# Local attention in a fused attention and expert kernel: the score products of two heads alternate, and a small add moves from VectorE to GpSimd

## The chip, the cores and the metric

The kernel runs on one core of a Trainium2 chip. The metric is device microseconds per execution; the time of a kernel is the median of several runs. In the profile PE is TensorE (PEld its weight loads), DVE VectorE, ACT ScalarE, POOL GpSimd and SP SyncE, whose queue issues the loads and copies.

## The reference, cut to what matters

Four batches of eight heads have 512 local and 32 global tokens, with 64 numbers per head. A local token attends to the 32 global tokens and to the local ones at most 32 places away; a global token attends to all. Two feed-forward stages follow.

```python
s_ll = scale * np.matmul(q_l, k_l.transpose(0, 1, 3, 2))
s_ll = np.where(np.abs(pos[:, None] - pos[None, :]) <= 32, s_ll, -1e9)
s_l = np.concatenate([scale * np.matmul(q_l, k_g.transpose(0, 1, 3, 2)), s_ll], axis=-1)
# sm(s): e = exp(s - max(s)); e / (sum(e) + 1e-9)
out_l = np.matmul(sm(s_l), np.concatenate([v_g, v_l], axis=2))
x = out.transpose(0, 2, 1, 3).reshape(2176, 512)
x = np.square(np.maximum(x @ w_in, 0)) @ w_out                 # first feed-forward
P = sinkhorn(softmax-like gate of x, 8 rounds)                  # 8 experts
out = sum over e of P[:, e] * (np.maximum(x @ w1[e], 0) @ w2[e])
```

Inputs and output are 32-bit floats; some of the attention's inputs are scaled up, so that the scores are large.

## The kernel before, in words

Every product is made of three: each operand is split into a rounded part (`hi`) and what is left (`lo`), and `split_terms` gives hi x hi, hi x lo and lo x hi, which TensorE adds up in PSUM.

The attention comes first, up to about 215 us. It goes over 16 items: a batch and a pair of heads. The two heads of a pair lie side by side on the partitions, head 0 on 0 to 63 and head 1 on 64 to 127 (`halves`). Each item has two local steps of two tiles of 128 queries each (`qp`), and every second item a global step for the queries of the global tokens of two pairs. So five steps make a period: local, local, local, local, global.

The order of the work is written out by hand: each engine does its instructions in the order in which the loop at L659 issues them. In turn `k` of that loop several steps are at different points. First comes `loc_normalise` of step k-2 (L491), then `loc_least` of step k-1 (masking, and the smallest negated score of each row, L469), then on ScalarE and VectorE the evacuations from PSUM that the turn before left behind (`evacuate_all`, L361; `hi` by ScalarE at L363 or L365, `lo` by VectorE at L368 or L370), `loc_exp` of k-1 (L483), `loc_values` of k-4 (L519), `loc_scores` of k (L458) and `loc_transpose` of k-2 (L506). In some turns there follow the transposes of the next item's keys and queries, `prep_v` (L426: GpSimd splits the values at L80 and L81, and copies go out on the queue of SP) and, every second item, `glob_queries` (L535: four copies on GpSimd, L121). Last, `step_side` works on the weights of the first feed-forward stage, a few operations of ScalarE, VectorE and GpSimd at a time (`double_words`, L98 to L108; `split_words`, L113 to L117).

What the change touches: `loc_scores` takes two PSUM tiles "s", one per head, from a pool of two. For each head it makes three products for each of the two tiles of queries, 12 in all, each with 64 rows, 128 queries and 224 keys (L466). `loc_exp` leaves four sums of exponentials in `st[:, 4:8]`. `loc_normalise` adds the constant 1e-9 to them (L493) and takes the reciprocal (L494), both on VectorE; GpSimd then scales the four blocks of exponentials in place (L497), which TensorE transposes later in the same turn.

There are 32 local steps, so L493 and L494 run 32 times and L466 384 times.

Of the kernel before, what the change touches and what calls it, by code (L numbers as in the profile page):

```python
# [9 lines left out]
F32 = mybir.dt.float32  # L10
# [3 lines left out]
ALU = mybir.AluOpType  # L14
# [4 lines left out]
EPS = 1e-9  # L19
# [3 lines left out]
def split_terms(hi_s, lo_s, hi_m, lo_m):  # L23


    return ((hi_s, hi_m), (hi_s, lo_m), (lo_s, hi_m))
# [3 lines left out]
def kernel(  # L30
# [15 lines left out]
    nc = tc.nc  # L46
# [4 lines left out]
    E, _, F2 = w1.shape  # L51
    P = 128
# [5 lines left out]
    SEG = P + 3 * WINDOW  # L58
# [199 lines left out]
    with ExitStack() as actx:  # L258
# [3 lines left out]
        pss = actx.enter_context(tc.tile_pool(name="pss", bufs=2, space=PSUM))  # L262
# [190 lines left out]
        halves = (slice(0, D), slice(D, 2 * D))  # L453
        s_t, e_t, pt_t, st_t, inv_t = {}, {}, {}, {}, {}
# [2 lines left out]

        def loc_scores(i, n, qp):  # L458
            q, kt = QT[n], KT[n % 3]
            s_t[i] = []  # L460
            for r in halves:
                s = pss.tile([P, 2, SEG], F32, tag="s", name="s")
                for t in range(2):
                    qt = 2 * qp + t
                    for x, (a, c) in enumerate(split_terms(q[r, 0, qt], q[r, 1, qt], kt[r, 0, qt], kt[r, 1, qt])):
                        nc.tensor.matmul(s[:, t, :], lhsT=a, rhs=c, start=(x == 0), stop=(x == 2))  # L466
                s_t[i].append(s)

        def loc_least(i, n, qp):  # L469
            e = ap3.tile([P, 2, 2, SEG], F32, tag="e", name="e")  # L470
# [19 lines left out]

        def loc_normalise(i):  # L491
            e, st = e_t[i], st_t.pop(i)
            nc.vector.tensor_scalar_add(st[:, 4:8], st[:, 4:8], EPS)  # L493
            nc.vector.reciprocal(st[:, 4:8], st[:, 4:8])  # L494
            for c in range(4):
                v = e[:, c // 2, c % 2, :]
                nc.gpsimd.tensor_scalar(out=v, in0=v, scalar1=st[:, 4 + c : 5 + c], scalar2=1.0, op0=ALU.mult, op1=ALU.mult)  # L497
# [161 lines left out]
        for k in range(len(steps) + 6):  # L659
            if k < len(steps):  # L660
                kind, n, qp = steps[k]
                first, second = kind == "l" and qp == 0, kind == "l" and qp == 1
                closing = steps[k + 1][:1] + steps[k + 1][2:] == ("l", 0) if k + 1 < len(steps) else False
            else:
                first = second = closing = False
            at(k - 2, loc_normalise, glob_normalise)
            if 0 <= k - 1 < len(steps):
                kd, m, mq = steps[k - 1]
# [9 lines left out]
            at(k - 1, loc_exp, glob_exp)  # L678
            at(k - 4, loc_values, glob_values, 1)
            at(k, loc_scores, glob_scores, 1)  # L680
            if len(steps) <= k < len(steps) + 4:
                step_early(2)
# [31 lines left out]
            if first and n == 15:  # L714
                add_part(share, 1, 0, "kg")
                t = share.tile([P, 3, 512], F32R, tag="kt1", name="w20")
# [5 lines left out]
            if k == len(steps):  # L722
                add_part(share, 3, 0, "vb1")
                t = share.tile([P, 3, 512], F32R, tag="kt2", name="w31")
# [350 lines left out]
    for u in range(U1):  # L1075
        if u and u < U1 - 1:
            prepare((u + 1) * UF)
        if u == U1 - 1:
            t = cv.tile([P, 6, 512], F32, tag="cv", name="t").rearrange("p a b -> p (a b)")[:, 0 : 8 * P]
            t = t.rearrange("p (i k f) -> p i k f", i=4, k=2)  # L1080
# [47 lines left out]
    for tb, (j0, nj) in enumerate(TBS):  # L1128
        n = nj * P // 2
        for u in range(NS):  # L1130
            s = tb * NS + u
# [57 lines left out]
```

## Time and profile before

| | us |
|---|---|
| median of 3 runs | 2042.18 (2038.86 to 2042.25) |
| the profiled execution's own time | 2037.85 |
| its span, first to last instruction | 2035.9 |

| engine | busy us | share of the span | instructions |
|---|---|---|---|
| PE | 1997.6 | 98% | 10820 |
| DVE | 1210.8 | 59% | 2398 |
| ACT | 807.9 | 40% | 1856 |
| POOL | 922.6 | 45% | 1071 |

The share is an average over stages: in the first tenth of the span the page gives VectorE nine tenths and more, afterwards about half. TensorE's clock was granted in full for nearly all of the span (0.992 on average). Matmuls are pipelined, and their ends are modelled, so a busy TensorE is not one at its peak.

### The profile page before, as it was taken

How to read it: one execution, taken by the hardware profiler on the slowest of the kernel's cores; microseconds unless marked ns; L12 is line 12 of the kernel's file. 1: busy time of each engine (PE TensorE's matmuls, PEld its weight loads, DVE VectorE, ACT ScalarE, POOL GpSimd, SP SyncE). 2: the span in 40 equal slices, each digit the busy share in tenths (PEclk: the TensorE clock that was granted, in tenths of full speed). 3: DMA queues.
4: the chain of work that ended last, by engine and by line, in shares of the span. 5: the costliest groups of instructions: out<-in, count | busy, mean ns of one | idle time of the engine just before them, and what ended most of it. 6: DMA issues, size and time to landing. Idle time of an engine off the chain costs nothing.

```text
span 2035.9 us, 29259 instructions
## 1 busy us (share of the span) xinstructions
PE 1997.6 (98%) x10820; PEld 1814.2 (89%) x10820; DVE 1210.8 (59%) x2398; ACT 807.9 (40%) x1856; POOL 922.6 (45%) x1071
## 2 busy tenths in 40 slices
PE   8998999999999999999999999999999999999999
PEld 7997798989998899888998998998989999999998
DVE  7999556666456654555546445546455655555554
ACT  6887443323133342333324423423333443333332
POOL 6555323223124354373453543545534555555553
PEclk8999999999989999999999999999999999999999
DMA  6665111111002122222222221222122322222221
GB/s 155 145 139 127 52 63 42 42 42 52 1 12 62 63 73 72 64 62 63 73 73 81 85 73 62 65 71 73 62 65 75 100 84 83 83 76 81 83 78 42
DMA packets 194542, 147.63 MB, mean 73 GB/s; under 512 B 96864, under 2 KB 165728, under 8 KB 194400
## 3 DMA queue, kind: packets, MB, share of 16 engines
q1 hardware_dynamic: 194400, 145.77, 24.8%
q8 instruction: 85, 1.39, 0.3%
q14 instruction: 57, 0.47, 0.1%
HBM read 130.83 MB, written 4.46 MB: 66 GB/s over the span
## 4 chain that ended last, share of the span: by engine, by line
PE 88%; DVE 8%; issue 1%; ACT 1%; DMA 1%; SPq 1%; POOL 0%; DVEq 0%; POOLq 0%; ACTq 0%
PE y L1050 36%; PE pa L987 18%; PE pd L987 9%; PE y L854 8%; PE h L246 8%; PE pb L987 5%; DVE e L476 1%; PE pv L529 1%; DVE xl L368 1%; DVE xl L997 1%; DVE al L368 1%; PE lg L783 1%; DVE z L1003 1%; DVE bl L368 1%; PE s L466 1%
## 5 line engine op out<-in xcount | busy, mean ns | idle before, releaser
L1050 PE MATMUL y<-w,xh 128*128 128x512 f32 (+1 forms) x2184 | 672.4, 389 | 0.0
L1050 PEld LDWEIGHTS y<-w,xh 128*128 128x128 f32 x2184 | 408.9, 188 | 82.4
L987 PE MATMUL pa<-xh,w 128*128 128x384 f32 (+1 forms) x1536 | 424.4, 329 | 4.2 <-DVE z L1003 4.0
L80 POOL TENSOR_SCALAR w<-raw 128x512 fp32r<-128x512 f32 x192 | 121.4, 632 | 672.3 <-PE y L1050 672.3
L1050 PE MATMUL y<-w,xl 128*128 128x512 f32 x1092 | 425.0, 389 | 0.0
L1064 DVE SCALAR_TENSOR_TENSOR acc<-y,prob,acc 128x512 f32<-128x512 f32 (+1 forms) x250 | 187.1, 748 | 277.7 <-PE y L1050 277.7
L987 PEld LDWEIGHTS pa<-xh,w 128*128 128x128 f32 x1536 | 278.9, 188 | 9.5 <-DVE z L1003 6.2
L1011 ACT COPY snaps<-pa 128x384 f32<-128x384 f32 (+1 forms) x96 | 44.1, 460 | 536.6 <-PE pa L987 536.6
L81 POOL TENSOR_TENSOR w<-raw,w 128x512 fp32r<-128x512 f32 x192 | 249.5, 1300 | 16.0
L987 PE MATMUL pa<-xl,w 128*128 128x384 f32 (+1 forms) x768 | 251.1, 327 | 0.0
L992 ACT ACTIVATE xh<-z 128x384 fp32r<-128x384 f32 (+1 forms) x288 | 146.4, 508 | 248.8 <-DVE z L1003 248.8
L1050 PEld LDWEIGHTS y<-w,xl 128*128 128x128 f32 x1092 | 205.3, 188 | 42.7
L1003 DVE TENSOR_TENSOR z<-pb,snaps 128x384 f32<-128x384 f32 (+1 forms) x96 | 51.4, 536 | 284.7 <-PE pb L987 282.9
L987 PE MATMUL pd<-xh,w 128*128 128x384 f32 (+1 forms) x768 | 218.8, 328 | 0.0
L854 PE MATMUL y<-hid,w 128*128 128x384 f32 (+1 forms) x960 | 191.5, 357 | 4.2 <-DVE hid L255 2.1
L854 PEld LDWEIGHTS y<-hid,w 128*128 128x128 f32 x960 | 171.8, 188 | 21.1 <-DVE hid L255 3.3
L997 DVE SCALAR_TENSOR_TENSOR xl<-z,xh 128x384 fp32r<-128x384 f32 (+1 forms) x288 | 183.9, 639 | 3.7
L246 PE MATMUL h<-xh,w 128*128 128x384 f32 (+1 forms) x640 | 184.3, 362 | 0.8 <-ACT rs L252 0.8
L987 PEld LDWEIGHTS pa<-xl,w 128*128 128x128 f32 x768 | 144.9, 189 | 1.8
L115 POOL TENSOR_TENSOR cv<-cv,w 128x512 f32<-128x512 f32 x32 | 47.9, 1503 | 214.5 <-ACT w L113 154.9
L987 PEld LDWEIGHTS pd<-xh,w 128*128 128x128 f32 x768 | 140.8, 189 | 0.0
L956 DVE TENSOR_TENSOR w<-tw,w 128x512 fp32r<-128x512 f32 x190 | 125.4, 699 | 9.0 <-ACT w L953 8.7
(184 smaller groups left out, 3260.1 us busy)
## 6 DMA issues: line engine op xcount, KB each, us to landing
raw<-in_moe_w_dram SPq DMA_DIRECT2D x192, 512.0 KB, 3.6
raw<-in_moe_w_in_dram SPq DMA_DIRECT2D x16, 512.0 KB, 3.9
raw<-in_moe_w_out_dram SPq DMA_DIRECT2D x16, 512.0 KB, 4.5
rqk<-in_k_l_dram SPq DMA_DIRECT2D x32, 128.0 KB, 2.6
rqk<-in_q_l_dram SPq DMA_DIRECT2D x32, 128.0 KB, 2.9
rv<-in_v_l_dram SPq DMA_DIRECT2D x32, 128.0 KB, 2.6
out_dram<-acc SPq DMA_DIRECT2D x15, 256.0 KB, 2.2
vb<-va SPq DMA_DIRECT2D x32, 112.0 KB, 3.2
```

The lines of the kernel that those rows point to most:

```text
L80: nc.gpsimd.tensor_scalar(out=hi, in0=src, scalar1=1.0, scalar2=0.0, op0=ALU.mult, op1=ALU.add)
L81: nc.gpsimd.tensor_tensor(out=lo, in0=src, in1=f32(hi), op=ALU.subtract)
L246: nc.tensor.matmul(ps, lhsT=w, rhs=x, start=(k == 0), stop=(k == 3 * NC - 1))
L368: nc.vector.tensor_tensor(out=lo, in0=ps, in1=f32(hi), op=ALU.subtract)
L854: nc.tensor.matmul(ps, lhsT=w, rhs=m, start=(f == 0 and x == 0), stop=(f == last and x == 2))
L956: nc.vector.tensor_tensor(out=dst(1, c, k), in0=src, in1=f32(dst(0, c, k)), op=ALU.subtract)
L987: nc.tensor.matmul(ps, lhsT=lhs, rhs=rhs, start=(first and t == 0), stop=(t == 5), skip_group_check=True)
L992: nc.scalar.activation(out=hh, in_=z, func=AF.Relu)
L997: nc.vector.scalar_tensor_tensor(out=hl, in0=z, scalar=0.0, in1=f32(hh), op0=ALU.max, op1=ALU.subtract)
L1003: nc.vector.tensor_tensor(out=z, in0=ps, in1=snap, op=ALU.add)
L1050: nc.tensor.matmul(ps, lhsT=lhs, rhs=rhs, start=(t == 0), stop=(t == 3 * UF - 1))
L1064: nc.vector.scalar_tensor_tensor(out=s, in0=ps, scalar=pr, in1=s, op0=ALU.mult, op1=ALU.add)
```

## The change

The two score tiles are taken first; then, for each tile of queries and each of the three terms, the product of head 0 is issued and behind it that of head 1. The add of the constant becomes an instruction of GpSimd, with a multiplication by 1.0 as its second operation; the reciprocal stays on VectorE.

```diff
         def loc_scores(i, n, qp):
             q, kt = QT[n], KT[n % 3]
-            s_t[i] = []
-            for r in halves:
-                s = pss.tile([P, 2, SEG], F32, tag="s", name="s")
-                for t in range(2):
-                    qt = 2 * qp + t
-                    for x, (a, c) in enumerate(split_terms(q[r, 0, qt], q[r, 1, qt], kt[r, 0, qt], kt[r, 1, qt])):
+            s_t[i] = [pss.tile([P, 2, SEG], F32, tag="s", name="s") for _ in halves]
+            for t in range(2):
+                qt = 2 * qp + t
+                pairs = [split_terms(q[r, 0, qt], q[r, 1, qt], kt[r, 0, qt], kt[r, 1, qt]) for r in halves]
+                for x in range(3):
+                    for s, terms in zip(s_t[i], pairs):
+                        a, c = terms[x]
                         nc.tensor.matmul(s[:, t, :], lhsT=a, rhs=c, start=(x == 0), stop=(x == 2))
-                s_t[i].append(s)
...
         def loc_normalise(i):
             e, st = e_t[i], st_t.pop(i)
-            nc.vector.tensor_scalar_add(st[:, 4:8], st[:, 4:8], EPS)
+            nc.gpsimd.tensor_scalar(out=st[:, 4:8], in0=st[:, 4:8], scalar1=EPS, scalar2=1.0, op0=ALU.add, op1=ALU.mult)
             nc.vector.reciprocal(st[:, 4:8], st[:, 4:8])
```

## Rows read from the trace of the kernel before

**Rows 1.** Windows of 21.2 us: busy us of PE, PEld, DVE, ACT, POOL; clock, DMA.
```profile
81.20:102.40 21.20, 20.89 (x180) 19.52 (x178) 20.60 (x72) 19.14 (x63) 11.61 (x25) 1.00 0.69 144
144.80:166.00 21.20, 20.87 (x180) 19.52 (x179) 20.63 (x72) 19.11 (x63) 11.64 (x25) 1.00 0.73 154
```
**Rows 2.** Waits of PE, 60 to 160 us: total us, times, longest.
```profile
PE pv L529 <- DVE xl L368: 1.3, 4, 0.4
```
**Rows 3.** Groups of VectorE, 0 to 204 us: count, busy us, mean ns, idle before.
```profile
L493 DVE TENSOR_SCALAR st<-st 128x4 f32<-128x4 f32 x32 | 10.4, 325 | 1.4 <-ACT e L487 1.3
```
**Rows 4.** Timeline of ScalarE and VectorE at two adds: start us, duration us.
```profile
64.95 0.19 ACT L487 ACTIVATION_READ_ACCUMULATOR e<-e,st 128x1 f32 x1
...
65.17 0.17 DVE L493 TENSOR_SCALAR st<-st 128x4 f32<-128x4 f32 x1
...
119.95 0.15 DVE L493 TENSOR_SCALAR st<-st 128x4 f32<-128x4 f32 x1
120.14 0.18 DVE L494 RECIPROCAL st<-st 128x4 f32<-128x4 f32 x1
```
**Rows 5.** Timeline of VectorE at one of six long adds.
```profile
115.92 0.68 DVE L493 TENSOR_SCALAR st<-st 128x4 f32<-128x4 f32 x1
116.64 0.18 DVE L494 RECIPROCAL st<-st 128x4 f32<-128x4 f32 x1
```
**Rows 6.** Timeline of GpSimd, 112.6 to 118 us, in the same period.
```profile
112.88 1.74 POOL L497 TENSOR_SCALAR e<-e,st 128x224 f32<-128x224 f32 x4 [3.06 <-PE ptb L515]
114.59 0.62 POOL L80 TENSOR_SCALAR va<-rv 128x512 fp32r<-128x512 f32 x1
115.30 1.28 POOL L81 TENSOR_TENSOR va<-rv,va 128x512 fp32r<-128x512 f32 x1
116.55 1.09 POOL L121 TENSOR_SCALAR bd<-qg 64x64 fp32r<-64x64 f32 x4
117.73 1.75 POOL L497 TENSOR_SCALAR e<-e,st 128x224 f32<-128x224 f32 x4
```
**Rows 7.** Groups of GpSimd by form, 0 to 204 us.
```profile
L497 POOL TENSOR_SCALAR e<-e,st 128x224 f32<-128x224 f32 x128 | 55.8, 456 | 65.4 <-PE pta L586 25.9 <-DVE st L494 12.4 <-PE ptb L515 11.9
...
L339 POOL TENSOR_SCALAR_AFFINE_SELECT mask<-mask 128x32 f32<-128x32 f32 x1 | 0.2, 213 | 0.0
```
**Rows 8.** Timelines of VectorE, ScalarE and GpSimd at two hand-overs to GpSimd.
```profile
112.51 0.18 DVE L494 RECIPROCAL st<-st 128x4 f32<-128x4 f32 x1
...
176.33 0.60 ACT L113 CAST w<-cv 128x512 fp32r<-128x512 f32 x1
...
177.01 1.27 POOL L115 TENSOR_TENSOR cv<-cv,w 128x512 f32<-128x512 f32 x1 [1.00 <-ACT w L113]
```
**Rows 9.** Timeline of VectorE: three more reciprocals.
```profile
44.46 0.18 DVE L494 RECIPROCAL st<-st 128x4 f32<-128x4 f32 x1
...
178.34 0.18 DVE L494 RECIPROCAL st<-st 128x4 f32<-128x4 f32 x1
...
190.28 0.18 DVE L494 RECIPROCAL st<-st 128x4 f32<-128x4 f32 x1
```
**Rows 10.** Timeline of GpSimd beside these three.
```profile
43.11 2.53 POOL L117 TENSOR_TENSOR w<-cv 128x512 fp32r<-128x512 f32 x2
...
178.36 1.29 POOL L117 TENSOR_TENSOR w<-cv 128x512 fp32r<-128x512 f32 x1
...
190.31 1.26 POOL L117 TENSOR_TENSOR w<-cv 128x512 fp32r<-128x512 f32 x1 [0.69 <-DVE st L493]
```
**Rows 11.** Waits of VectorE, 24 to 34 us.
```profile
DVE cv L100 <- ACT cv L98: 2.9, 2, 1.5
```
**Rows 12.** Timeline of PE: the twelve score products of two steps.
```profile
102.60 1.25 PE L466 MATMUL s<-kt,q 64*128 64x224 f32 x12
...
170.07 1.55 PE L466 MATMUL s<-kt,q 64*128 64x224 f32 x12
```
**Rows 13.** Waits of PE, 195 to 225 us.
```profile
PE y L854 <- POOL w L117: 0.9, 1, 0.9
```

## The prediction

> **What bounds the kernel now.** I read the span and the busy shares first, then the stretch that the diff touches, then who waits there. Both edits lie in the local part of the attention stage, from about 8 to 190 us of a span of 2035.9 us; what follows is bound by TensorE and doesn't see them, except that it starts later or earlier. The attention stage is periodic: five steps (four local ones, one global) every 21.2 us. In one such period TensorE, VectorE and ScalarE are all nearly full: 20.9, 20.6 and 19.1 us, GpSimd only 11.6 [rows 1]. So busy shares don't decide, and I went to the waits. From 60 to 160 us TensorE has a wait for VectorE in nearly every period, 1.3 us in four of them, while the waits view of VectorE for the same stretch has no row at all [rows 2]: what is missing to 21.2 us in VectorE is the gap of some 0.03 us between instructions. VectorE sets the pace there. A microsecond that VectorE loses or gets back between 30 and 215 us is therefore a microsecond of the kernel, as long as no other engine takes over; that is the basis of the sum.
>
> **The add moves to GpSimd: what VectorE gets back.** The 32 adds of L493 cost VectorE 10.4 us, 0.33 us on average [rows 3], but that mean hides two kinds. Most take 0.15 to 0.17 us, and from the add's start to the reciprocal's 0.19 or 0.20 us pass (119.95 to 120.14 [rows 4]). Six times, once per period, the add takes 0.68 to 0.70 us (115.92 [rows 5]): it ends at 116.60, with GpSimd's subtraction of L81 (115.30 + 1.28 = 116.58 [rows 6]). Three others are long or lie beside GpSimd's work for the weights (below).
>
> The Trainium skill has the rule for this ("SBUF — State Buffer", SBUF: two separate sides): some VectorE instructions and GpSimd's share a pair of ports that one of them holds for its whole instruction. The trace agrees (the add ends 0.02 us after the subtraction). By that rule alone, moving the add would win some 0.5 us at each such place and nothing would stand against it; the rows below say what does.
>
> **What the move costs.** The chain was exp (ScalarE), add, reciprocal (VectorE), scaling (GpSimd). It becomes ScalarE, GpSimd, VectorE, GpSimd: two more hand-overs, and VectorE's reciprocal, with all of VectorE's work behind it, now waits until GpSimd has reached the add in its own order. Prices: no row shows a 128x4 operation on GpSimd. Its cheapest neighbour by size is 0.21 us (128x32), the scaling with scalars read from a tile is 0.46 (128x224) [rows 7]; I take 0.20, since the smaller one is nearest, with 0.10 and 0.46 as ends. ScalarE to GpSimd takes 0.08 us (176.93 to 177.01), VectorE to GpSimd 0.19 (112.69 to 112.88) [rows 6, 8]; GpSimd to VectorE isn't in the trace, I take the 0.03 of ScalarE to VectorE (65.14 to 65.17 [rows 4]), with 0.19 as the upper end. GpSimd's own next instruction with a wait starts 0.09 us after the last (117.64 to 117.73 [rows 6]). So behind busy GpSimd the reciprocal starts 0.09 + 0.20 + 0.03, about 0.33 us after the work ahead of it.
>
> *Where GpSimd has a backlog.* In the regular period GpSimd, once released by the previous reciprocal, has four scalings, the split of the values (L80, L81) and four copies (L121) queued ahead of the next add: from 112.88 without a break to 117.64 [rows 6]. The reciprocal would start at 117.97 in place of 116.64 [rows 5]: 1.33 us later, the freed 0.72 us already set against it. GpSimd's backlog starts from the reciprocal before, so it moves with VectorE and isn't caught up. Six periods: 8.0 us. The same beside the weights: at 44.46 the copies of L117 last to 45.64, so 45.97, 1.5 us later; at 178.34 they last to 179.65, 1.6 us; at 190.28 to 191.57, 1.6 us [rows 9, 10]. The add at 184.8, between them, I put at -0.3 by estimate: VectorE is late by 1.6 us then, and one of its side operations is no longer held up by GpSimd. Sum: 8.0 + 1.5 + 1.6 + 1.6 - 0.3 = 12.4 us.
>
> *Where GpSimd is idle.* Of the other 22 adds, three lie before 25 us. There the reciprocals come up to 1.6 us later, but VectorE then waits 2.9 us for the landing of the first weights, whose loads are issued ahead of this [rows 11]: 0, upper end 1.6. For 19 GpSimd does the add while VectorE still works through the evacuations before it, if exp ended 0.31 us (0.08 + 0.20 + 0.03) before VectorE arrives. In ten it does; in nine it ends later, at the extreme with VectorE's arrival (65.14 against 65.17 [rows 4]). There the reciprocal would come 0.31 after exp in place of 0.23, a loss of up to 0.1 us, unless exp itself comes earlier.
>
> **The score products alternate.** The instructions are the same 12 per step; only their order and the release of the two score tiles change. Twelve take 1.25 us in the regular steps and 1.55 in a few [rows 12]: the two heads, which lie on different halves of the rows, overlap already in part. Alternating, all twelve can overlap: at best half of 1.55, so the gain is between nothing and 0.47 us a step; I take 0.28, the middle. Both heads now need both score buffers free, while the second head's came half a microsecond later; VectorE's reading of them ends before the products start, so I cost this at nothing. TensorE isn't the pace, so 0.28 us doesn't go into the sum itself. What it does is bring exp earlier through transposes and ScalarE, and with that the nine late adds are hidden too. So 19 x 0.19 = 3.6 us come back; without any gain in the products it is 10 x 0.19, 1.9 us at most.
>
> **Sum.** 12.4 - 3.6 = +8.8 us on the profiled execution, whose own time is 2037.85 us: 2046.7. The median of the runs shown, 2042.18, lies 4.3 us above that execution, so I forecast 2051.0. Ends: with an add of 0.10 us the ten backlog places lose 1.0 less. With 0.46 and a slow hand-over (0.43 more per place) they lose 4.3 more and the nine late adds some 4 more, plus 1.6 at the start and 0.5: about +19. At the seam with the next stage TensorE still waits 0.9 us for GpSimd's weight copy [rows 13]; this chain moves with VectorE, but up to 3 us could be lost in it.
>
> **Rivals.**
> *TensorE sets the pace (faster).* For it: TensorE's share of a period, 20.9 us, is the highest [rows 1], and the chain of waits goes through it once a period. Then VectorE's stalls fall into TensorE's shadow and 32 x 0.28 = 9 us come back: 2033. Against it: VectorE has no wait [rows 2]. It would decide if VectorE had slack for the stall of 1.3 us in each period. The Trainium skill ("TensorE: Matmul & The Clock Gate", Part 3, The mechanism) has matmuls finish in program order, so that the old order could overlap only where the head changes and the new one everywhere; by that rule the gain per step would be nearer 0.6 us, and this rival 2023. The 1.25 against 1.55 us speaks against it: half of the overlap is there already.
> *The hand-over is dear.* Each place costs its upper end: 2061. For it: the scaling's 0.46 us and the 0.19 us from VectorE to GpSimd. Against it: the scaling has 56 times the columns.
> *The stall is absorbed.* The waiting VectorE lets ScalarE and TensorE run ahead, and the freed adds and the seam give back all but 0 to 4 us: 2042 to 2046. For it: three engines are nearly balanced. Against it: VectorE has nothing to catch up with, it was never idle.
> *The products don't overlap better than before.* Then only the 1.7 us above are missing: 2053, within the forecast's own range.
>
> **Chances.** Forecast (with the last rival) 0.63, 2046 to 2056; dear hand-over 0.12; absorbed 0.14; TensorE sets the pace 0.11. A measurement of this kernel tells 0.2%, 4.1 us, from no change. Slower by more: 0.75; within: 0.15; faster: 0.10. The range for 8 in 10 leaves out the fast rival and half of the dear one: 2043 to 2060.
>
> **What would show it.** Right, if the profile after has, once per period, a reciprocal that VectorE waits some 1.9 us for, ended by GpSimd's add, right behind the four copies; if the period is about 22.0 us; if the twelve products take about 0.97 us; if the stage from 217 us on is the same, only later. Wrong, if VectorE's wait there is short, if the period shrinks, if the add takes over 0.4 us, or if TensorE's waits for VectorE vanish.

## The result and the profile after

| | before | after |
|---|---|---|
| median, same chip, us | 2042.22 | 2055.39 (2046.36 to 2056.47, 6 runs) |
| the profiled execution's own time, us | 2037.85 | 2046.36 |
| its span, us | 2035.9 | 2044.6 |
| last local reciprocal at, us | 190.28 | 198.59 |
| first outputs of the feed-forward stage at, us | 217.35 | 225.81 |

The changed kernel is slower: the ratio of the times is 1.0063, 95% interval 1.0034 to 1.0092. (One of the six runs of the kernel before took 2459.65 us; the ratio leaves it out.) The two profiled executions differ by 8.5 us. By the last local reciprocal 8.3 us have arisen, and the first feed-forward stage starts 8.46 us later. That the end lies about as much later is in part chance: behind that stage the difference first shrinks and then grows again, in waits of the last layer that the kernel before doesn't have ("The time", below).

The windows of one period each in the profile after (the columns of [rows 1]). The period has become 22.13 us. Each engine is now further from full than in [rows 1], VectorE by more than two microseconds, and only GpSimd has more to do:

```profile
79.90:102.03 22.13, 20.51 (x180) 18.49 (x179) 19.41 (x69) 19.07 (x62) 12.33 (x28) 1.00 0.69 144
102.03:124.16 22.13, 20.52 (x180) 18.50 (x178) 19.39 (x69) 19.07 (x62) 12.35 (x28) 1.00 0.64 132
```

The waits of VectorE after, from 60 to 170 us: total us, times, longest. Before, there was no row here. There are two waits in a period, one of 1.9 us and one of 0.4 us:

```profile
DVE st L496 <- POOL st L495: 11.5, 10, 1.9
```

The timeline of GpSimd after, around the long wait (start, duration; in brackets the idle time before and what ended it). From the release at 115.76 GpSimd works without a break through the scalings, the split of the values and the copies, as in [rows 6]; the add (L495) stands behind all of it:

```profile
115.76 1.73 POOL L499 TENSOR_SCALAR e<-e,st 128x224 f32<-128x224 f32 x4 [0.38 <-DVE st L496]
117.47 0.62 POOL L80 TENSOR_SCALAR va<-rv 128x512 fp32r<-128x512 f32 x1
118.17 1.27 POOL L81 TENSOR_TENSOR va<-rv,va 128x512 fp32r<-128x512 f32 x1
119.41 1.09 POOL L121 TENSOR_SCALAR bd<-qg 64x64 fp32r<-64x64 f32 x4
120.58 0.19 POOL L495 TENSOR_SCALAR st<-st 128x4 f32<-128x4 f32 x1
```

VectorE in the same stretch. It was done at 118.90 and starts the reciprocal at 120.81, 0.04 us after the add's end by the rounded rows (0.03 in the unrounded ones):

```profile
118.22 0.68 DVE L368 TENSOR_TENSOR bl<-ptb,bh 96x512 fp32r<-96x512 f32 x1
120.81 0.18 DVE L496 RECIPROCAL st<-st 128x4 f32<-128x4 f32 x1 [1.91 <-POOL st L495]
```

The groups of the add and the reciprocal after, 0 to 216 us (columns of [rows 3]). The 10.4 us of adds [rows 3] are off VectorE, but in the whole stage it waits 24.8 us for 6.2 us of adds:

```profile
L495 POOL TENSOR_SCALAR st<-st 128x4 f32<-128x4 f32 x32 | 6.2, 193 | 47.0 <-ACT e L489 46.1
L496 DVE RECIPROCAL st<-st 128x4 f32<-128x4 f32 x32 | 5.6, 174 | 24.8 <-POOL st L495 24.8
```

The score products after, on TensorE's timeline (against [rows 12]): 0.93 us in a regular step, but 1.30 us in the step behind a global one.

```profile
105.70 1.30 PE L469 MATMUL s<-kt,q 64*128 64x224 f32 x12
109.39 0.93 PE L469 MATMUL s<-kt,q 64*128 64x224 f32 x12
```

### The profile page after: what moved, and what is told of

Its sections match the earlier page's. It is cut to its first block, busy times and chain, and to the rows that moved or that the text cites. A ratio compares the mean times of both kernels' runs of the same rounds, so it can differ in the third digit from the quotient of the medians.

```text
span 2044.6 us, 29288 instructions
## 1 busy us (share of the span) xinstructions
PE 1994.8 (98%) x10820; PEld 1806.6 (88%) x10820; DVE 1200.9 (59%) x2366; ACT 807.8 (40%) x1856; POOL 927.0 (45%) x1103
## 4 chain that ended last, share of the span: by engine, by line
PE 86%; DVE 7%; ACT 2%; POOL 2%; issue 1%; DMA 1%; SPq 1%; DVEq 0%; POOLq 0%; ACTq 0%
PE y L1052 36%; PE pa L989 17%; PE pd L989 9%; PE y L856 8%; PE h L246 8%; PE pb L989 5%; DVE xl L999 1%; DVE z L1005 1%; PE lg L785 1%; DVE e L478 1%; ACT e L489 1%; PE pv L531 1%; POOL e L499 0%; POOL va L81 0%; DVE xl L368 0%
## 5 line engine op out<-in xcount | busy, mean ns | idle before, releaser
L80 POOL TENSOR_SCALAR w<-raw 128x512 fp32r<-128x512 f32 x192 | 120.8, 629 | 673.5 <-PE y L1052 673.5
L81 POOL TENSOR_TENSOR w<-raw,w 128x512 fp32r<-128x512 f32 x192 | 248.9, 1296 | 16.0
L856 PEld LDWEIGHTS y<-hid,w 128*128 128x128 f32 x960 | 171.7, 188 | 21.1 <-DVE hid L255 3.3
```

What stands on the lines that cost most here:

```text
L80: nc.gpsimd.tensor_scalar(out=hi, in0=src, scalar1=1.0, scalar2=0.0, op0=ALU.mult, op1=ALU.add)
L81: nc.gpsimd.tensor_tensor(out=lo, in0=src, in1=f32(hi), op=ALU.subtract)
L856: nc.tensor.matmul(ps, lhsT=w, rhs=m, start=(f == 0 and x == 0), stop=(f == last and x == 2))
```

## The experiments

The theory: one edit alone costs, the add, and it costs because of what stands ahead of it in GpSimd's order; neither the hand-overs nor the add itself are dear, and alternation is worth little while VectorE sets the pace. The rivals: the hand-overs, the alternation, or TensorE as the bound. Each time is compared with runs of the kernel before on the same chip: a median of 2037.17 us for each edit alone, the copies issued early and the add on ScalarE; 2038.53 for the two idle operations, the two kernels without the constant and the old order behind a global step; 2037.55 for the repetition and the cleared queue; 2039.61 for the last.

### Each edit alone

Only the alternation, the add back on VectorE:

```diff
-            nc.gpsimd.tensor_scalar(out=st[:, 4:8], in0=st[:, 4:8], scalar1=EPS, scalar2=1.0, op0=ALU.add, op1=ALU.mult)
+            nc.vector.tensor_scalar_add(st[:, 4:8], st[:, 4:8], EPS)
```

> Only the order of the score products changes; the add stays on VectorE. Theory (the add's place in GpSimd's queue makes all of the loss, and VectorE sets the pace): the last reciprocal of a local step starts at 189.5 to 190.5 us, against 190.28 before and 198.59 with both changes, and the time is within 0.1% of the kernel before. Rival 1 (alternating costs by itself, because both score tiles have to be free before the second product): the last reciprocal at 193 us or later. Rival 2 (TensorE sets the pace): 183 us or earlier, since 28 of 32 steps save some 0.3 us on TensorE.

Measured: 2038.79 us, ratio 1.0001 [0.9986, 1.0017]; last reciprocal at 188.74, a little earlier than expected. Its window shows why nothing moves: TensorE has 0.7 us less to do than in [rows 1], and VectorE nearly as much (20.50 against 20.60).

```profile
80.00:101.07 21.07, 20.20 (x180) 18.36 (x179) 20.50 (x73) 19.21 (x63) 11.57 (x25) 1.00 0.70 147
```

Only the add on GpSimd, with the old order of the products:

```diff
-            s_t[i] = [pss.tile([P, 2, SEG], F32, tag="s", name="s") for _ in halves]
...
+            for r in halves:
+                s = pss.tile([P, 2, SEG], F32, tag="s", name="s")
```

> Only the add moves to GpSimd; the score products keep the order of before. Theory (queue on GpSimd): the last reciprocal at 198.5 to 200.5 us, the time 8 to 10 us above before in the profile, with one wait of VectorE of 1.9 us per period. Rival 1 (alternating costs by itself): 191 to 195 us, the rest of the loss being the other edit's.

Measured: 2047.74 us, ratio 1.0052 [1.0035, 1.0070]; last reciprocal at 199.07, the same two waits of 1.90 and 0.40 us per period. The loss is the add's alone.

### What the add waits for

First the four copies L121 issued a turn earlier, so that the add no longer stands behind them:

```diff
-                if n % 2:
-                    glob_queries(n)
+            if first and n % 2:
+                glob_queries(n)
```

> Both changes, but the four copies of glob_queries on GpSimd are issued one turn earlier, where GpSimd is idle, and so no longer stand ahead of the add (1.09 us of the queue). Theory (queue): VectorE's wait once per period falls from 1.9 to 0.8 us, six periods give back 6 x 1.09 = 6.5 us, and the last reciprocal starts at 191 to 193 us in place of 198.59. Rival (the hand-overs between the engines are the cost, whatever is queued): 197.5 us or later.

Measured: 2042.84 us, ratio 1.0024 [1.0012, 1.0037]; last reciprocal at 192.30. The wait falls by about the copies' 1.09 us and no more, from 1.91 to between 0.85 and 0.88, since L80 and L81 still stand ahead:

```profile
99.06:120.21 21.15, 20.29 (x179) 18.45 (x178) 19.45 (x69) 19.09 (x62) 12.34 (x28) 1.00 0.67 138
```

Then the reverse, two idle operations more on GpSimd behind the add, so that the hand-over lengthens by their time:

```diff
+            nc.gpsimd.tensor_scalar(out=st[:, 4:8], in0=st[:, 4:8], scalar1=1.0, scalar2=0.0, op0=ALU.mult, op1=ALU.add)
+            nc.gpsimd.tensor_scalar(out=st[:, 4:8], in0=st[:, 4:8], scalar1=1.0, scalar2=0.0, op0=ALU.mult, op1=ALU.add)
```

> Both changes, and two operations of the same size (a multiplication by one in place) stand on GpSimd ahead of the add, as a doubled and tripled hand-over. Each costs 0.19 us and some 0.08 us to the next. Theory (VectorE waits for GpSimd's queue, and has no slack): the wait once per period grows from 1.9 to 2.4 us, the one of 0.39 to 0.9 us, a third of some 0.5 us appears; the period grows from 22.1 to 23.6 us and the last reciprocal from 198.59 to 206 to 210 us. Rival (part of the wait is a latency that hides more work): less than 203 us.

Measured, one run: 2065.72 us; last reciprocal at 211.35, above the expected range. The waits grew about as expected (1.9 to 2.5 us, 0.4 to between 0.57 and 1.06), and the undisturbed period, 23.47 us, is near the expected one; the third wait that was expected did not come. Two periods took over a microsecond more than the others, and at their start TensorE's clock fell to 1.2 GHz for 3.4 us. The first of these rows is one of the two; its granted clock is 0.97 and TensorE's busy time 1.6 us higher than in the second, a period without the fall:

```profile
83.22:108.06 24.84, 21.98 (x185) 20.00 (x184) 19.75 (x68) 19.08 (x62) 13.89 (x36) 0.97 0.62 130
108.06:131.53 23.47, 20.40 (x180) 18.28 (x179) 19.69 (x68) 19.21 (x62) 13.89 (x36) 1.00 0.59 120
```

### The add elsewhere, or nowhere

The add on ScalarE, as an activation with the constant as bias:

```diff
-            nc.gpsimd.tensor_scalar(out=st[:, 4:8], in0=st[:, 4:8], scalar1=EPS, scalar2=1.0, op0=ALU.add, op1=ALU.mult)
+            nc.scalar.activation(out=st[:, 4:8], in_=st[:, 4:8], func=AF.Copy, bias=EPS)
```

> The products alternate, and the add is done by ScalarE right behind the four exponentials of the step: no queue of another engine, and VectorE is rid of 10.4 us. Theory: no wait of VectorE over 0.5 us per period; VectorE's period falls from 21.2 towards 19.9 us, but ScalarE, with 19.1 + 4 x 0.2 us, is then full as well: a period of 20 to 20.5 us, the last reciprocal at 183 to 187 us, the time 3 to 7 us below before. Rival (three engines are balanced, so nothing comes back): 189.5 us or later, the time as before.

Measured: 2038.56 us, ratio 0.9995 [0.9982, 1.0007]. The stage gains 3.6 us (last reciprocal at 186.70, as expected), 3.0 of them behind 173.9 us, after the last regular period. The period does not gain: 21.27 us, where 20 to 20.5 was expected. ScalarE now has 19.89 us of work in it, and VectorE waits for the add three times in a period (60 to 160 us):

```profile
DVE st L496 <- ACT st L492: 4.6, 14, 0.4
```

The next two leave out the constant. (The largest exponential of a row is 1, so its sum is at least 1, and 1e-9 is below what a 32-bit float resolves there.) First with alternation:

```diff
-            nc.gpsimd.tensor_scalar(out=st[:, 4:8], in0=st[:, 4:8], scalar1=EPS, scalar2=1.0, op0=ALU.add, op1=ALU.mult)
             nc.vector.reciprocal(st[:, 4:8], st[:, 4:8])
```

> The products alternate and the add of the constant 1e-9 is left out altogether (the sums are at least 1, so it would not show in 32 bits). Theory (VectorE sets the pace until it is relieved by some 1.3 us a period, then ScalarE and the chain through TensorE do): no wait of VectorE for GpSimd; a period of 19.9 to 20.6 us against 21.2 before; the last reciprocal at 181 to 185 us against 190.28 before; time 5 to 9 us below before. Rival (the three engines are so balanced that VectorE's relief turns into new waits, as with the add on ScalarE): a period of 21 us or more, the last reciprocal at 186 us or later.

Measured: 2032.06 us, ratio 0.9964 [0.9949, 0.9978], faster than both kernels; last reciprocal at 181.38. Then from the kernel before, so without the alternation:

```diff
-            nc.vector.tensor_scalar_add(st[:, 4:8], st[:, 4:8], EPS)
             nc.vector.reciprocal(st[:, 4:8], st[:, 4:8])
```

> The add is left out as in the run beside it, and the score products keep the order of before. Theory: once VectorE is relieved, TensorE (20.9 of 21.2 us busy before) is what the alternating order helps; here the period stays at 20.5 to 21.0 us and the last reciprocal at 184 to 187 us, 2 to 4 us later than with the alternating order. Rival (alternating is worth nothing, relieved or not): the same as the run beside it, within 1 us.

Measured: 2035.73 us, ratio 0.9993 [0.9979, 1.0007]; last reciprocal at 185.61. The period, 21.12 us, is longer than expected. The windows, first of the kernel with alternation, then of the one without: in the second TensorE is busy for 21.10 of 21.12 us and sets the pace alone.

```profile
95.89:116.32 20.43, 20.07 (x179) 18.39 (x178) 19.61 (x68) 19.08 (x63) 11.62 (x24) 1.00 0.69 143
```
```profile
97.95:119.07 21.12, 21.10 (x179) 19.75 (x178) 19.62 (x68) 19.07 (x63) 11.62 (x24) 1.00 0.69 141
```

So before there were two limits, VectorE's at 21.2 us and TensorE's at 21.1. Alternating alone or leaving out the add alone takes away one and wins about 0.1 us per period (21.07 and 21.12), both win 0.8 (20.43).

### The products behind a global step

The changed kernel, with the products in the old order only in the step behind a global one:

```diff
+            if i and steps[i - 1][0] == "g":
+                order = [(j, t, x) for j in range(2) for t in range(2) for x in range(3)]
+            else:
+                order = [(j, t, x) for t in range(2) for x in range(3) for j in range(2)]
```

> Both changes, but a local step that follows a global one keeps the old order of its products. Theory (there the second product waits for the tile that ScalarE's exponentials of the global step still read, so that twelve products take 1.30 us; with the old order the first head's six run ahead): these products take 1.25 us or less, VectorE's wait of 0.39 us once per period falls to 0.1 to 0.35 us, and the last reciprocal starts 0.3 to 1.5 us earlier than 198.59. Rival (that wait isn't due to the score tile): 0.39 us as before.

Measured, one run: 2048.09 us; the short wait stays at 0.37 to 0.39 us, so the rival held. By the single instructions the old order takes 1.28 to 1.30 us there, not the 1.25 or less that was expected, and the new one about 1.30, so there was nothing to win back by the order. The last reciprocal, at 199.99, is 1.4 us later than in the changed kernel, not earlier; 1.2 us of this have arisen by the fourth reciprocal, before the first step that the edit touches. What the tile's release is worth by itself was not tried.

### How firm the result is

The changed kernel once more, with no edit:

> The changed kernel once more, to see how firm its difference is. Theory (the queue of GpSimd): the trace shows the same waits again, 1.9 us and 0.4 us once in each period, the last local reciprocal at 198 to 199.5 us, and the profiled execution 8 to 9 us over that of the kernel before where no further half-clock stretch of TensorE falls between 520 and 670 us. The median lies 8 to 14 us above before (ratio 1.004 to 1.007), according to how many executions have those stretches. Rival (chance placement of the run): below 1.003.

Measured: 2051.57 us (2047.0 to 2056.47, 6 runs), ratio 1.0068 [1.0047, 1.0088]. The waits and the last reciprocal (198.69) are the same as in the first profile. The time is not: this profiled execution took 2054.05 us, the first one 2046.36. Of the 7.7 us, 4.9 have arisen by the start of the next layer (613.14 and 618.04 us), the rest later, and both run the same instructions there. The windows from 520 to 640 us, first of the first profile, then of this one: TensorE is as busy, but its granted clock was 0.94 there and is 0.89 here.

```profile
520.00:640.00 120.00, 116.58 (x643) 110.14 (x642) 64.09 (x122) 34.28 (x64) 26.87 (x24) 0.94 0.06 16
```
```profile
520.00:640.00 120.00, 116.94 (x616) 111.41 (x614) 57.53 (x104) 30.69 (x57) 26.56 (x24) 0.89 0.04 14
```

### A queue that is cleared

If the queue is the price, the two edits must win once nothing stands ahead of the add. The split of the values is issued one turn earlier for odd items, and the copies two:

```diff
-            if second:
+            if second and n % 2 == 0 or first and n % 2:
                 prep_v(n)
-                if n % 2:
-                    glob_queries(n)
+                if n == 1:
+                    glob_queries(1)
+                elif n and n % 2 == 0:
+                    glob_queries(n + 1)
```

> The changed kernel with the two GpSimd operations that stand ahead of an addition in the regular period issued one and two turns earlier. Theory (the queue is the price, the hand-overs are not): the wait of 1.9 us per period vanishes (0.4 us or less is left), the period is 20.5 to 20.9 us, the last local reciprocal lies at 182 to 188 us, and the time is 2 to 7 us below before, so the two edits gain once the queue is clear. Rival (the hand-overs themselves, or new waits for the values now copied earlier): a period of 21.15 us or more as with the copies early, the last reciprocal at 191 us or later, and a time not below before.

Measured: 2043.64 us, ratio 1.0022 [1.0008, 1.0037]; last reciprocal at 191.76. Half of it held. The period fell to 20.70 us, with waits of 0.5 us at most, so the hand-overs are cheap:

```profile
99.37:120.07 20.70, 20.06 (x178) 18.38 (x177) 19.45 (x68) 19.05 (x63) 12.34 (x28) 1.00 0.64 129
```

But outside the regular stretch the moved work and the split of the weights now stand ahead of three other adds, and VectorE waits 3.58 us for the reciprocal at 46.51, 3.71 at 179.50 and 1.70 at 191.76 (2.42, 2.84 and 1.70 us in the changed kernel). Of the 6.1 us of the median only 1.5 have arisen by the last reciprocal; behind the first outputs this profile has 34 us of TensorE at half clock, that of the kernel before 20. GpSimd ahead of the second:

```profile
174.63 0.62 POOL L80 TENSOR_SCALAR va<-rv 128x512 fp32r<-128x512 f32 x1
175.33 1.27 POOL L81 TENSOR_TENSOR va<-rv,va 128x512 fp32r<-128x512 f32 x1
176.57 1.29 POOL L115 TENSOR_TENSOR cv<-cv,w 128x512 f32<-128x512 f32 x1
177.93 1.27 POOL L117 TENSOR_TENSOR w<-cv 128x512 fp32r<-128x512 f32 x1
179.28 0.19 POOL L495 TENSOR_SCALAR st<-st 128x4 f32<-128x4 f32 x1
```

So, last, these three adds alone go back to VectorE:

```diff
+            eng = nc.vector if sum(s[0] == "l" for s in steps[:i]) in (4, 29, 31) else nc.gpsimd
-            nc.gpsimd.tensor_scalar(out=st[:, 4:8], in0=st[:, 4:8], scalar1=EPS, scalar2=1.0, op0=ALU.add, op1=ALU.mult)
+            eng.tensor_scalar(out=st[:, 4:8], in0=st[:, 4:8], scalar1=EPS, scalar2=1.0, op0=ALU.add, op1=ALU.mult)
```

> The kernel with the queue cleared, and the three additions that there still stood behind work of GpSimd's own queue (reciprocals at 46.51, 179.50 and 191.76 us, waits of 3.58, 3.71 and 1.70 us) put back on VectorE; the other 29 stay on GpSimd. Theory (only the queue ahead of the addition costs, place by place): the three waits fall to 0.8 us or less each, the period stays at 20.7 us, the last local reciprocal comes 7 to 9 us earlier, at 183 to 185.5 us, and the time is 3 to 6 us below before: the edits gain, with the constant kept. Rival (what the three waits held back is late for other reasons, as GpSimd's scaling there stands in the same queue): the last reciprocal at 189 us or later and a time within 2 us of before or above it.

Measured: 2034.92 us, ratio 0.9981 [0.9966, 0.9996]: with the constant kept, below both kernels, but below the one before by hardly more than what can be told from no change; the interval just leaves out 1. The three waits are gone and the period is 20.70 us. The last reciprocal, at 186.88, is later than expected by 1.4 us, because the first of the three waits only moved on by one step: the scalings of that step (L500) still stand behind the copies L117, and the next add behind the scalings. GpSimd's timeline there:

```profile
43.63 2.52 POOL L117 TENSOR_TENSOR w<-cv 128x512 fp32r<-128x512 f32 x2
46.12 1.75 POOL L500 TENSOR_SCALAR e<-e,st 128x224 f32<-128x224 f32 x4
47.83 0.63 POOL L80 TENSOR_SCALAR va<-rv 128x512 fp32r<-128x512 f32 x1
48.54 1.30 POOL L81 TENSOR_TENSOR va<-rv,va 128x512 fp32r<-128x512 f32 x1
49.93 0.19 POOL L496 TENSOR_SCALAR st<-st 128x4 f32<-128x4 f32 x1
```

VectorE there, with the wait:

```profile
50.15 0.18 DVE L497 RECIPROCAL st<-st 128x4 f32<-128x4 f32 x1 [2.83 <-POOL st L496]
```

## Why the prediction was right, and where its terms were off

**The backlog.** This was the term that decided, and it held. In the six regular periods the reciprocal behind the copies falls back by 1.24 to 1.27 us against the one before it (1.33 forecast), 7.5 us together in place of 8.0. Beside the weights the three places cost 1.40, 1.61 and 1.54 us (1.5, 1.6 and 1.6), and the one between them gives 0.38 (0.3). Together 11.7 in place of 12.4.

**The prices that no row had.** The add took 0.193 us (0.20), GpSimd to VectorE 0.03 (0.03), and the add starts 0.08 to 0.09 us behind busy GpSimd (0.09). The dear hand-over is excluded by the group's mean and by the cleared queue. The wait was 1.9 us and the period 22.13 (22.0).

**What comes back.** Forecast 3.6 us, measured 3.4: 8.3 at the last reciprocal less 11.7. But it is made otherwise, so the agreement is luck. The alternation was to bring 1.7 of the 3.6 us; with the add alone, in the old order, the last reciprocal lies only 0.5 us later (199.07), and the short wait is the same 0.4 us. At the start, costed at nothing, 0.75 us are won by the fourth reciprocal (32.42 to 31.67). In the step behind a global one, where 0.19 us was to come back, up to 0.1 is lost: there VectorE waits 0.4 us. The step of the forecast that failed is "VectorE's reading of them ends before the products start": in that step a score tile also serves the global step before, and it is ScalarE's exp (L571) that still reads it. ScalarE's timeline after, and the row of what TensorE's weight loads for the score products wait for, 60 to 170 us:

```profile
105.33 0.59 ACT L571 ACTIVATE e<-s,st 128x384 f32<-128x384 f32 x1
105.80 0.22 ACT L571 ACTIVATION_READ_ACCUMULATOR e<-s,st 128x1 f32 x1
```
```profile
PEld s L469 <- ACT e L571: 0.9, 5, 0.2
```

The first product starts at 105.70, the second, of the other head, only at 106.07 (by the single instructions). So the twelve need 1.30 us, exp isn't earlier, and the add isn't hidden. In the old order they need 1.28 to 1.31 us there when the add is on GpSimd, so the forecast's gain is missing in just these steps. That the release is what costs it is the reading of the trace; no run took it away.

**The alternation.** In a regular step, 18 of the 32, the twelve take 0.93 us (0.97 forecast): the products of the two heads start 0.01 us apart, and the gain is 0.32 us. By the rule of the Trainium skill ("TensorE: Matmul & The Clock Gate", Part 3, The mechanism) that was weighed there it would have been about 0.6 by estimate; the traces stand against it, since before, too, half of the overlap was there: the second head's first product starts at 102.92 us, ahead of the first head's fourth at 103.03 (by the single instructions).

**Who sets the pace.** VectorE did, as argued, and the rival in which TensorE's shadow swallows the stalls fell. But TensorE's limit was only 0.1 us behind, which the forecast did not see; it matters for nothing in this result, and for all that could be won.

**The seam.** Hardly anything was lost at the seam (8.3 us at the last reciprocal, 8.46 at the first outputs, row below against 217.35 before), and the products of that stage take the same 383.3 us in both profiles.

```profile
225.81 1.42 PE L856 MATMUL y<-hid,w 128*128 128x512 f32 x5 [1.30 <-ACT rs L252]
```

**The time.** The profiled execution was to rise by 8.8 us and rose by 8.5, and this agreement, too, is in part luck. The forecast's "what follows is bound by TensorE and doesn't see them, except that it starts later or earlier" did not hold for the last layer. Two instructions of VectorE there, before and after, come 5.82 and 8.73 us later:

```profile
1582.38 0.75 DVE L1064 SCALAR_TENSOR_TENSOR acc<-y,prob,acc 128x512 f32<-128x512 f32 x1 [1.97 <-PE y L1050]
2032.67 0.48 DVE L1064 SCALAR_TENSOR_TENSOR acc<-y,prob,acc 128x256 f32<-128x256 f32 x1 [0.95 <-PE y L1050]
```
```profile
1588.20 0.75 DVE L1066 SCALAR_TENSOR_TENSOR acc<-y,prob,acc 128x512 f32<-128x512 f32 x1 [1.97 <-PE y L1052]
2041.40 0.48 DVE L1066 SCALAR_TENSOR_TENSOR acc<-y,prob,acc 128x256 f32<-128x256 f32 x1 [0.95 <-PE y L1052]
```

Between the first outputs and the first of them the difference shrinks from 8.46 us by 2.6. The kernel before ran TensorE at half clock for 20 us in that stretch, the changed one for 17; half of the 3.4 us between them is 1.7 us, and the rest is not explained. Between the two instructions the difference grows by 2.9 us: TensorE waits four times for VectorE, and each time some 0.7 us are lost. These are the waits of TensorE and of its weight loads after, 1580 to 2030 us; before, there is no row:

```profile
PE pa L989 <- DVE z L1005: 2.1, 4, 0.5
PEld pa L989 <- DVE z L1005: 3.2, 4, 0.8
```

The forecast had these 2.9 us at nothing. The repetition has the same waits, and so have the add alone, the copies issued early and the old order behind a global step; no other profile has them, and three of those others have the add on GpSimd, too. What brings them about stays open.

The median rose by 13.2 us, and by 14.0 when it was taken again. At an equal granted clock the executions lie 11 to 12 us apart: at 0.991 over the whole they took 2036.4 us before and 2047.2 us changed on average (19 and 2 runs, all chips taken together), at 0.988 2042.6 and 2054.7 us (16 and 4 runs). That is near the 8.4 us of the attention and the 2.9 us of the last layer together. The runs of the changed kernel fall into two groups, 2046 to 2049 and 2054 to 2057 us, and its two profiles are one of each. Behind the first outputs TensorE ran at half clock for 17 us in the first of them and for 31 us in the second; the 14 us between them cost about half of that, 7 of the 7.7 us. Why the longer stretches come as often as they do here stays open.

## What to carry to other kernels

An instruction given to an engine with half its time free costs nothing only if that engine stands idle when it is wanted: read what is queued ahead of it, in order, and add that to the wait of the engine that takes the result. When two engines are nearly full, an edit that relieves one is worth what the other leaves over; undo or do each edit alone and both together before calling either useless. A queue that is cleared in the regular period must be looked at again at its two ends. A stage that an edit doesn't touch must be read in both profiles, too, before its time is called unchanged.

## What was not expected of the hardware

Two products on different halves of the rows run fully side by side when issued in turn (0.01 us apart, twelve in 0.93 us), and half so when issued head by head (1.25 us). Behind a global step the second head's first product started 0.37 us after the first head's, which was then already running.

TensorE's clock falls to half while it is busy without a pause. Windows of the second profile of the changed kernel: from 505 to 531.7 us TensorE is busy for all of 26.70 us at 2.4 GHz (1.00), and for the next 3.4 us, as busy, at 1.2 GHz (0.50).

```profile
505.00:531.70 26.70, 26.70 (x135) 22.69 (x135) 13.23 (x19) 8.00 (x14) 3.90 (x5) 1.00 0.06 21
531.70:535.10 3.40, 3.40 (x10) 2.63 (x9) 0.00 (x0) 0.42 (x1) 0.00 (x0) 0.50 0.00 0
```
